# A layer's forward and backward pass on one core: the last stores on SyncE's queue, and the sines of the transform constants ahead of the exponential of dt

## The chip, the cores and the metric

The kernel runs on one core of a Trainium2 chip. The core has five engines, each with its own list of instructions that it works through in order: PE (TensorE, matmuls into PSUM), DVE (VectorE), ACT (ScalarE, with tables of functions that an instruction of its own loads), POOL (GpSimd) and SP (SyncE, which here only issues DMAs). Engines wait for each other through semaphores. DMAs are issued by SP, by ACT and by POOL; the profile counts what SP and ACT issue under the hardware queues and what POOL issues under the software queue.

The metric is the device time of one execution in microseconds, as the median of several runs. A trace of one profiled execution tells what each engine did; its span runs from the first to the last instruction.

## The reference

`A_u` is x, 2048 rows of 512 in bf16. It is normalised, run through a state space layer (a long convolution, computed by Fourier transforms) and gated by a feed-forward block; the kernel returns the output and the gradients of it towards eleven inputs.

```python
def _A_ref(u, A_re, A_im, B_re, B_im, C_re, C_im, log_dt, Dskip):
    dt = jnp.exp(log_dt)[:, None]
    A, Bc, Cc = A_re + 1j * A_im, B_re + 1j * B_im, C_re + 1j * C_im
    P = jnp.exp((dt * A)[:, :, None] * l[None, None, :])
    K = jnp.einsum("dn,dnl,dn->dl", Cc, P, dt * Bc).real
    # y = causal convolution of u with K along the rows, by rfft and irfft over 2L
    return y + u * Dskip[None, None, :]

def _B_ref(x, w1, w2):
    return silu(x @ w1) @ w2

xn = _layernorm(A_u)
out = A_u + _A_ref(xn, ...) * silu(_B_ref(xn, w1, w2))
# returned: out, and by jax.vjp with grad_out the gradients of
# A_u, A_re, A_im, B_re, B_im, C_re, C_im, log_dt, Dskip, w1, w2
```

## The kernel before

The function `body` (line 1488) writes the whole program down once in a plain order, through a recorder; nothing is issued yet. A plan then cuts it into 3232 steps (a step is one instruction, or a few matmuls of one group) and puts them into the sequence that is packed in the string `ORDER` (line 185): `solve` (line 421) unpacks it, `emit` (line 119) issues the steps in that sequence, and `tie` holds each engine to it. A number of `ORDER` also says whether a copy out of PSUM, or a row of the normalisation, runs on ACT or on DVE (the steps made with `any_copy` and `any_affine`). The order on each engine and each DMA queue is therefore written out by hand, step by step, and the line that issues nearly everything is one: line 171 of `emit`. That is why almost every row of the profile says L171. Line 1684 opens and closes the program; its rows are drains and semaphores.

**The start.** SP loads x (four pieces `x_sb` of 512 KB, `load_x`), the weights `W1` and `W2` (1792 KB each) and six parameters (`par_Ar`, `par_Ai`, `par_Br`, `par_Bi`, `par_Cr`, `par_Ci`, 128 KB each, by transposing DMA). ACT issues the loads of log_dt (`ldt`) and of Dskip (`Dbc`). Three chains begin there and share DVE:

- `make_consts` (line 546) makes the constants of the transform. `twiddles` multiplies two integer ramps into `prod` on DVE (a multiply and an addition, for each half) and ACT takes the sine into `TF`. PE transposes `TF` into `pt_t`, eight blocks at a time, and a copy brings each eight to `TI`; there are four such groups.
- `ssm_magnitudes` (line 801) takes dt = exp(ldt) on ACT, multiplies it with `par_Ar` on DVE (`lam` and the four parts of `lamr`), and takes 30 exponentials of `lam` and `lamr` on ACT into `mag_all`. SP stores that as eight blocks `Md` and later loads it back, block by block, as `mag`, where `gen_tables` needs it.
- `layer_norm` (line 656) takes the statistics of x on DVE (`st`, `mv`, `ve`), a power on POOL (`rstd`) and scales the rows (`xn`). Two rows at a time are transposed on PE and copied to `XT` on DVE, and with `XT` the feed-forward block begins: matmuls with `W1` into `ps_h`, copied out to `hT` by ACT or DVE, `aT` = silu on ACT, matmuls with `W2` into `ps_o`.

**The end.** The last stretch weaves three things: the gradients of `W2` and `W1` (`gen_dw2`, `gen_dw1`: matmuls into `ps_w`, copies to `o`, stores), the state space parameters' gradients of the last block, and the backward pass of the normalisation.

- `gen_ssm_grads` (line 1219) runs once for each of four blocks of 128 channels, in the order `k.back = 3, 0, 1, 2`, so block 2 is last. It computes six gradients into `gout` on DVE, transposes them on PE (`pt_g`), copies them back on ACT, and stores them in six pieces of 32 KB (line 1268). Then it stores the gradient of log_dt (`ddt`).
- `gen_ln_bwd` (line 1437) goes through the rows in eight pairs of 128, in the order `first` = 5, 6, 7, 0, 1, 2, 3, 4. For each it loads the incoming gradient `Gt` on SP, multiplies and adds on DVE, and stores `Gt`, 256 KB, at line 1475. Four buffers hold `Gt`.
- `gen_dw1` ends with four parts of the last piece of `W1`'s gradient, each of which is copied by ACT and stored on SP (`out_dram<-o`, 64 KB).

All other stores go through `k.st`, which is POOL's queue (line 1522): in the end six stores of `gout`, `ddt`, the last pieces of `o` and the `Gt`.

Of the kernel before, what the change touches and what calls it, by code (L numbers as in the profile page):

```python
# [180 lines left out]
class Plan:  # L181
# [1 line left out]

    ROOM, BOUND = 212832, 450.0
    ORDER = (
        "c-l>v4`|eBddHvVo!RL)J3BW!H#;}X&P}skI-8rF=5jWd%Vx7#n+s{0rfHg{Y3ijCLJ*NOwN`>i5D^<h775!RvMeIout?a7UAD4_h!v3_vWNt+RwOKTS"
# [3 lines left out]
        "x>*zQuyS2c$Ds)38bVgfPy-(kg>qxgo>z7vT(>K}g8f^_Zi|~9!?m)wGTek9EmN)1x`O{}|Rleg|Vc$0SxvZn#EUSMd=j0Eeg!}+o=IDD$vwIc`p2QQ5"  # L190
        "@s#0P9_xR>3TL>lqU}%Q8`>)C|Fe87|B9}2jK76U_vHxOe=bwHAwR;_XW_8`kLxn0O;AdH%&Z$SgPu$qJvy&;A4d}-I;#&Qtykds0lIu3c}9IJS$r-B4"
        "_VowTePhAWe@GK1bPedy>#jKGOe5Ss%+O9nz#TJeASC`Qy%MMe?HIrUAjxVbSG_xHo@H!#^;gnO=K(~Q4{wfZB;HySubncC0k+40sUI9=zTo^CGq_=9e"
        "}Sd;6AH+;nMW?Df?u&C*-0g#6~6L0RC0<w>BBooGu~dlD0B8!5V8ikEa~g<Gdy0YUtHtdIBGsm7Q{yzM1eQcA6#*TUp_BI85I+I;K_mTbYo-kYMg+yuL"
        "|Vh>|(2@U&U%YWH|VCv_V7(D^os%MxDo{A-yu4hIKyS#RrU=u4hIz&EdJXZTi2$bJQ>6Tx^qq7sh4MILX>Gxx`|gnX!<>OOi`(1%6lnQ%%^@x9?o30c%"
        "dRzDfCvJf(k2KJ?&ozLq%Jrbt04=m{So<8TQ1MlsI-X+#%bRjH+E*S_NvOS!4Y)BzT3h!Fib<KrbSl6!56|&(1D}SOR09X?INTQc3ZpD9-Q&I`1u;nRv"
        "s2_7pghHs(BYbU83I6XwD_V9fp2SXNz89UEXeHi`Vr@eKyY9zIXPvwK^u$G6yLa?u{9!{k7%4IxjMEgrnGA9Hn7-}o^-P~>a7nM|2vHjY4Nbo(zV)+8h"
        "h#&QXN%at&H_gPFQ|oDc&Z<%@s(rtvX(;+-(Q1@AW|NG*)E5WA`=X$Ucw^_VmdcYPho?T!Dc?j|10vRXuFS{he4{Gm|d5#Q&vvHWfwTI6@LB^ttWZwkW"
        "Q}c+yht@mq~Eyu<iln5_s#1F6fl(Ag(^rZE!FRHqYq}?uIi*`8ElegkzBDX@n+dG$#k~w?VW~05Sd(%_U_=*h5ssv3~&$s_>OV60_qfZ8$6tLxZ6|Y$I"
        "OI%D<z%G{_X#s|7OTOn?Xp`6sehvl&5_@bM+^%<SAIjbDLW(XgdOuEoBfmja%7N;B}B;z{Jb?nWzd_Y>nLj-GDwzMZdzEeW|nv)=@ooF-P1zKhBF-#X("
        "qPB`}^c>4g$P3VOCq>VX7Myhz89AK3iNZ(Eld{6d4bu2o=*AhB^o&B0Ua>n4RA|r5^1-JhKZz-bbKFIh>ql+G>UwXAy4@p0ntB0}OuJcazZO4k8P!l$`"  # L200
        "43{L^b!t0W*-oC^&R&!BZI_DTr&`iB>}jYmPL50?<CxO~JN;H((n;2RRevpi4ets0J!GoE-3IqtXf!1+d;ZI?=Z0hHE$00fJS6eB0oU(Uve71=8FMZE{"
        "6#zlq<u}Qk*0!2$1997e@@XhvEFs)`DnAuDYwvJS)?tn%K{jYL^BoWGLp`aCwI!6>}J&8v;OO}A$Iu@e5F}^KpW_D8_u_~!xFqMK!>23>+2WtHas36pK"
        "QTGTfpx))@_I0VucJ<PTcTV|4x3wdT+QlcIi7hftIUS^(C@*Qh(+cW7Nv?A7~0|JfXV!-myD@cDA}ljX(p$sKw$i^^4Ube?oi0w_jnCoAM=@`8WPuXyz"
        "f;U5{N(Z)4LgVq=h+=pEilAm1|H&<V2TxSIDjNzM`3Y7T2weY}B&%;TFFXMUE6@T~}MS^VpkBYVzqybP_;QfSir`kD;kql1omle8x6@HfoKz;DLu#zr3"
        "M^{aVIipVITS&LPR`X1)g;qGnMWd$ui&sM?pW4bH5Ph`QFA&;K|Ynd%=g%SBnua5c|(c`vBfQ=nom9PKN@D-><e#&zlzi7uR+QC<=wf4}ea24R^DD*xw"
        "h2Kmg%_aKA$m!=<>(@xN-=!I5&ImqSqVln<KZuPQUVE1BXCSMiK88LeBCT#-gpN92f%^D;>gZ$mnjyu4BgY~uuX<bMInFwVS*7Y8Xy|5|n5SNw=e|Uxy"
        "$gG#>7T_<H+=6!G4xG<Ux6=im$UBp*ubY9R7s}YK$X-lJM{urix!KNomQDi#<}h!XYO|Wn$~iz^Emxxjg&`XTFlz5_*tvR$tw4hXO?!~)BM1=tNF+jBe"
        "sDy2au?l{hR5@!_yGjn}gpX>)*$^1-K}|Wr0{sxFkt-!w<p93FeRcm=gWxeAO(xr(EAD`o_5y-M`X&zt8Fx4aW@w;mh!^H_C5GU$+iA<ULQexMZ7ou11"
        "t{Y)HFi;<PUOv6p)pkIf^i$(ZL1P^9noxehVA1-XjM75V}gQSc}!`8qpkR_P8>mAAS@CZHNS4tpg(%J;xqKQ=gm#>;Tr#g4X*tuhap3?1-qK5ckk^ZeT"
        "C=v!yCX1uEAvekTtl4Da}gd~q?C6}ipmcb37=iEkH;M7hk1?CN6sX=_*IIx<e$)nw>jTS>y*R7q7`nayjtHiCHk51BCmk$40bp7Rdw>o>#@q0pt`BHXW"  # L210
        "8<IT~tFoGy{W9z3oLjT)7`|M_ud9wZX_vg>r^6OT=g~;svFLTjytLOQt?nUPJdf5~s}t~L)pOb{VqSa4@wEbf=Bq`Y-M~u2vku2KleE>JvVKyUbZmLe`"
        "LOyR9U;zh>M<<!jBNI`N}|olxUT!md;X=$2*dm=TC?i5<kSpR82yCNBOtHUi{_z+u+l;7GUqtG3o7{OGf!UnA!O(~jhs`ilbY+!qUa~AbH;J9H{!@*Cx"
        "<55Bjnvgf2Yed=IiA>!Z%~>J~+v+cF|9LHiq*J^FZ5>W2chm0@LmQGt8H)8hEaUE<D|QeVVV0`Z42k^B!9#L1fFN?eJ0ub!yD~f$R6E=eaYC9D=5yIa)"
# [1475 lines left out]
```

## Time and profile before

| | us |
|---|---|
| median of 3 runs | 556.71 (556.11 to 558.98) |
| the profiled execution, its own time | 558.34 |
| the profiled execution, its span | 556.3 |
| PE busy, of the span | 514.4 |
| DVE busy | 514.9 |
| ACT busy | 432.8 |
| POOL busy | 69.8 |

The granted TensorE clock is 0.989 over the span. Busy time of PE is modelled from the starts of pipelined matmuls, so a busy PE isn't one at its peak. Register, branch, semaphore, drain and DMA-issuing instructions of the queues count as idle. A row of the timeline gives start, duration, engine, line, operation and what it writes and reads; "SPq" and "ACTq" are the issues of those engines' queues. In brackets stands how long the engine had been idle and what ended the wait.

### The profile page before, as it was taken

What the parts mean: (1) busy time and instruction counts of PE and PEld (TensorE: products, weight loads), DVE (VectorE), ACT (ScalarE), POOL (GpSimd) and SP (SyncE); (2) the same over time, 40 slices, a digit from 0 to 9 for tenths busy, and PEclk for the clock granted to TensorE, in tenths of its full rate; (3) what the DMA queues carried; (4) which work ended last, traced back from release to release, by engine and by line L of the source; (5) the groups of instructions that cost most, each with busy time, mean ns of one, the idle gap of its engine ahead of it and who ended that gap; (6) DMA issues with size and microseconds to landing.
All of it is one profiled execution on the core that took longest, in us unless ns stands there. A gap on an engine that the chain in (4) does not pass through costs nothing.

```text
span 556.3 us, 18980 instructions
## 1 busy us (share of the span) xinstructions
PE 514.4 (92%) x8173; PEld 368.1 (66%) x8173; DVE 514.9 (93%) x930; ACT 432.8 (78%) x707; POOL 69.8 (13%) x133
## 2 busy tenths in 40 slices
PE   0799989999979889879999999999999999999995
PEld 0566556767647657567686777777665667667774
DVE  8899998999989999999999999868999898899994
ACT  6999897999888869999999998564556656676533
POOL 3241210110000100000000000000000120403333
PEclk9999998999979999999999999999999999999999
DMA  8687775889897999967679977999999999999993
GB/s 269 222 334 194 264 281 182 257 292 230 206 290 237 229 351 338 192 187 134 209 248 227 333 236 265 230 256 238 270 228 235 237 241 225 234 219 235 246 222 138
DMA packets 169140, 134.41 MB, mean 242 GB/s; under 512 B 115552, under 2 KB 149088, under 8 KB 166496
## 3 DMA queue, kind: packets, MB, share of 16 engines
q1 hardware_dynamic: 162704, 115.36, 81.0%
q0 software_dynamic: 6064, 17.57, 8.8%
q8 instruction: 64, 1.05, 0.7%
q10 hardware_dynamic: 288, 0.26, 0.2%
q14 instruction: 20, 0.16, 0.1%
HBM read 49.28 MB, written 56.10 MB: 189 GB/s over the span
## 4 chain that ended last, share of the span: by engine, by line
PE 69%; DVE 14%; ACT 10%; issue 3%; DMA 3%; POOL 0%; ACTq 0%; DVEq 0%; POOLq 0%
PE ps_w L171 15%; PE ps_da L171 9%; PE ps_dx L171 9%; PE ps_i L171 8%; PE ps_h L171 6%; PE ps_s L171 5%; PE ps_o L171 5%; ACT dA L171 3%; PE ps_k L171 3%; PE psS L171 3%; PE pt_t L171 3%; DVE AR L171 2%; DVE YD L171 2%; DMA h_in<-Hd 2%; PE ps_v L171 2%
## 5 line engine op out<-in xcount | busy, mean ns | idle before, releaser
L171 PEld LDWEIGHTS <-W 128*128 128x128 bf16 x1008 | 92.2, 99 | 27.2 <-issue 4.4
L171 ACT CAST dA<-ps_s 128x512 bf16<-128x512 f32 x151 | 83.0, 627 | 9.0 <-PE ps_s L171 6.7
L171 ACT CAST Vb<-ps_v 128x320 bf16<-128x320 f32 x113 | 40.7, 441 | 34.4 <-PE ps_v L171 24.6
L171 PE MATMUL ps_h<-XT,W 128*128 128x256 bf16 x448 | 61.8, 284 | 0.9 <-DVE XT L171 0.7
L171 PE MATMUL ps_o<-W,aT 128*128 128x512 bf16 x224 | 60.3, 386 | 0.9 <-ACT aT L171 0.7
L171 PE MATMUL ps_da<-doT,W 128*128 128x256 bf16 x448 | 58.2, 273 | 0.0
L171 PE MATMUL ps_dx<-W,dhT 128*128 128x512 bf16 x224 | 58.1, 379 | 0.0
L171 PE MATMUL ps_w<-YD,a_tok 128*128 128x512 bf16 x224 | 56.6, 379 | 0.7 <-ACT o L171 0.7
L171 PEld LDWEIGHTS <-xn 128*128 128x128 bf16 x512 | 46.7, 98 | 14.5 <-DVE xn L171 4.5
L171 PE MATMUL ps_w<-dh_tok,xn 128*128 128x256 bf16 x448 | 56.0, 273 | 0.0
L171 DVE TENSOR_TENSOR Tp<-Vb,Eb 128x1280 bf16<-128x1280 bf16 x64 | 51.3, 818 | 2.5 <-ACT Vb L171 1.6
L171 ACT CAST dB<-ps_i 128x512 bf16<-128x512 f32 x82 | 44.1, 621 | 5.7 <-PE ps_i L171 5.7
L171 PEld LDWEIGHTS <-TF 128*128 128x128 bf16 x416 | 28.1, 99 | 19.9 <-ACT TF L171 11.4
L171 DVE TENSOR_TENSOR dhT<-ps_da,dhT 128x512 bf16<-128x512 f32 x56 | 37.2, 685 | 4.2 <-PE ps_da L171 2.0
L171 PEld LDWEIGHTS <-YD 128*32 128x32 bf16 (+1 forms) x2112 | 25.0, 103 | 16.5 <-issue 14.5
L171 ACT CAST o<-ps_w 128x512 bf16<-128x512 f32 (+1 forms) x30 | 16.4, 559 | 23.6 <-PE ps_w L171 11.8
L171 ACT CAST hT<-ps_h 128x512 bf16<-128x512 f32 x49 | 28.5, 622 | 5.5 <-PE ps_h L171 5.3
L171 PE MATMUL ps_s<-dB,F 128*64 128x512 bf16 x192 | 29.7, 396 | 2.6 <-DVE dA L171 1.3
L171 PE MATMUL ps_k<-W,YD 128*32 128x20 bf16 x2048 | 26.2, 204 | 5.7 <-issue 5.3
L171 PEld LDWEIGHTS <-aT 128*128 128x128 bf16 x224 | 19.3, 98 | 17.6 <-issue 4.1
L171 PEld LDWEIGHTS <-a_tok 128*128 128x128 bf16 x224 | 20.1, 98 | 16.3 <-issue 0.6
L171 POOL DMA_DIRECT2D Hd<-hT x16 | 14.1, 884 | 130.5 <-ACT hT L171 126.1
(234 smaller groups left out, 1162.8 us busy)
## 6 DMA issues: line engine op xcount, KB each, us to landing
Yd<-YD SPq DMA_DIRECT2D x8, 1024.0 KB
Ed<-E SPq DMA_DIRECT2D x8, 640.0 KB
Eb<-Ed SPq DMA_DIRECT2D x8, 640.0 KB
h_in<-Hd SPq DMA_DIRECT2D x10, 512.0 KB
Hd<-hT POOLq DMA_DIRECT2D x8, 512.0 KB, 6.7
dhT<-Hd SPq DMA_DIRECT2D x8, 512.0 KB
DHd<-dhT SPq DMA_DIRECT2D x8, 512.0 KB
Md<-mag_all SPq DMA_DIRECT2D x8, 480.0 KB
```

The lines of the kernel that those rows point to most:

```text
L171: getattr(getattr(nc, engine), op)(*[on(a) for a in args], **{w: on(a) for w, a in kw.items()})
```

## The change

Two stores get another queue, and the sequence is another one in two places. The packed string is new as a whole; its lines can't be read, so only its first and last are shown, and what is in it follows as lists.

```diff
     ORDER = (
-        "c-l>v4`|eBddHvVo!RL)J3BW!H#;}X&P}skI-8rF=5jWd%Vx7#n+s{0rfHg{Y3ijCLJ*NOwN`>i5D^<h775!RvMeIout?a7UAD4_h!v3_vWNt+RwOKTS"
...
-        "L!sUZu>@FY}hjEXWp!1wViMhuIGeTq#4(5{6*exitg#?%$1CA$i^fiUPb;FsX9pN"
+        "c-l>v4`|eBddHvVo!Pl@c6N4lc6M%<olfVxbS^hL&F0cHm(AsJHkYQkG-thBnx<YVX$TS|4c1CnB!~nFR*ofz?1?NA77-Co?6N0|h*%L3k!7(W)-EDew"
...
+        "EP96f%jRowH?|9<$PDR8-arNNIE*_Bc#cCMiF=YCjGSAyur)3j>Y}-#SLk5bnvyB77@2Y^Y_01-%Pj"
     )
@@ gen_ssm_grads
     for i in range(6):
-        k.st(k.outs[2 + i][bs, :], outb[:, i])
+        (nc.sync.dma_start if b == k.back[-1] else k.st)(k.outs[2 + i][bs, :], outb[:, i])
@@ gen_ln_bwd, rows
-        k.st(k.o1_v[:, 2 * c:2 * c + 2, :], Gt[:])
+        (nc.sync.dma_start if c in first[-2:] else k.st)(k.o1_v[:, 2 * c:2 * c + 2, :], Gt[:])
```

**The first 331 steps** are the same set in another order; the start of each engine's list:

```
ACT before: ldt, Dbc | dt=exp | TF=sin | TF=sin | 25 x mag_all=exp | hT | 5 more mag_all ...
ACT after:  ldt, Dbc | TF=sin | TF=sin | dt=exp | TI<-pt_t | 25 x mag_all=exp | hT | 5 more mag_all ...

DVE before: p_h p_t p_t pj | prod kk prod | sh kq kq | prod prod | pj st | lamr sh lam kq mv lamr st lamr mv lamr
            | st p_e st mv sp_dBr mv | TI<-pt_t | st st mv mv ve ...
DVE after:  prod prod prod | p_t p_h | prod | p_e p_t | st kk mv sh st kq pj mv sh kq pj st kq st kf mv mv
            | lam st lamr lamr lamr lamr ecst mv st maskf ve | mv sp_dBr st ...

SP before:  x_sb Ar x_sb Br Ci x_sb Bi W1 Cr x_sb W2 Ai | 8 x Md, then mag
SP after:   x_sb x_sb Ar x_sb Br x_sb W1 Bi Ai Cr Ci W2 | 8 x Md, then mag

PE before:  TF group | xn group | TF group | 12 steps of ps_h | xn group | TF group ... | TF group
PE after:   TF group | TF group | TF group | xn group | 10 steps of ps_h | xn group | a step of ps_h | TF group ...
```

The new sequence puts five steps on the other engine of the two: a copy of `TI` (DVE to ACT), a row of `xn` (ACT to DVE), and three copies of `hT` (two ACT to DVE, one DVE to ACT; one of the two that come to DVE stands behind the row `AR<-ph,ecst`). PSUM buffers are handed out by the sequence, so many tiles get another number of the same eight.

**The end.** Behind step 331 the sequence is the same but for the six stores of `gout` of the last block, which now stand directly behind ACT's copy of `gout`. With the new queues, the lists end so:

```
SP before:   ... dh_tok | Gt load (c=3) | Gt load (c=4) | o | o | o | o
SP after:    ... dh_tok | 6 x gout | Gt load (c=3) | Gt load (c=4) | Gt store (c=3) | o | o | o | o | Gt store (c=4)
POOL before: ... gout o o gout o gout Gt Gt ddt o gout Gt gout Gt gout
POOL after:  ... o o o Gt Gt ddt o
```

More of the change, by code (lines that the diff above doesn't have):

```diff
@@ L190 @@
[L190 to L213, printed above, removed]
@@ new lines @@
+        "=SFT3R<IUxTft=cW$QX4HYN7>7&|0zRo`T;T;4alE6<#bq{OI53Sh<;n;OPQs14z2ab9W6>ha+0T1<*1hBp8Q7Vbx?l5_?^gJktJ=BC$g7WF4K2HbMk$"
+        "7zlkO$bV85lCfTLCGzopl+;NTTq-5nTnwdb4IcY<#y!<hoe#x^>Tl5kCIe80>T&LGPbY7OCwrhiNC0f?yqCAu@c&kVTT^6N7y0Bw`dESPz4C4#*ZAF8x"
+        "(ktr{T;rL6vWz-_XPlBxC<o-9(bzHUe1`RJW98q<A+5k!oYmjNzAb3%807&nPU{0{hm*Ygn|v3aD8kP*iZE+l2DPL&<WuA}UUuo4?9{Aof!64iN25j7$"
+        "YZHTl2uXTDk~k@p=EtY|A$Bxs4d7>(xYF=v~JX^vQ6vqIo^3e3bf^r{idwzy1$=i{0`lrJvvL-u2rn`l>T|-{GO!Y>;yGw)=eYpWhv`rHE+wItvvF4p;"
@@ new lines @@
+        "z>w?uC+YcTI=j>l0mo>)mjfrr&8bt>w_iMNNqHO5jWTu!nuM%c$mb1qoNQjj;*lxTXtu;eLIeuY_C;{rVnWkkC2&>MV6L;d}VaG<I)ehLd4Gb-&j!t;y"
+        "fw5yK(D*o}Bk75l|y9$QrTvZwvWBRYmHruC@vZ4{RkozWMqWy&}l?9;<~M^8eZ@_tB<>kaJ=kF<pBSCBdpjK>2i;Q(CZWdX~U<qtf<kLqcCm)hg#qr%E"
+        "(!m6%n-u)>{`?4-G`>~Lf#gJiavt^K#&+9!s5T<kh?;Z4-0q3gA@t{|JEI*PNT?~t%M}|U|YzyaU>murtl(TY6Z)q;%!Y%CyJs}$|F!KrB5`^|TrB$xD"
+        "6@QC&R>CT_T$LyKA<sl8ga$Q2Ym-Xw|2cG=*flL4!%k(|i%wPdV3C7ZJCEPla}QQJ>)h?3CNARIy{j+d5BK%H8fH!h<1_{6Btu+2q;4B)J=f<NT+%DLg"
@@ new lines @@
+        "?Nq;*{0tVZG+6xCD~BpJ%Qf@Ru(u4ctJhX!!!LrjjtS|4{JH}(f$Thlpn&AVeAr8WP-)`OL$~KOy|bwDmFM4Y~(urUy+}o?EzNa4D#m0?0OhGW#uGX_J"
+        "FaQ;O8IFy5U<FsMrI7bP;#mtUO7??$=$i3m#|D+@em&cH-&--3kZOpy#|A*4IFTgS1UTCgB)ldfGw}$Ebby+c4TF$hYNR(Ogothh0Qf9QzmGpr(d>FFE"
+        "#~qHGR}#L#dU3|onpv+^%!FU<}VSgRGPK?x8cA^)U@!6f^w;NvUup4+)S+RX~=7EN1P<XY?tdNDLy)eJnRcoTW3JJCwq{lvJ5qo+H3Z==<)B_W?t>^Ff"
+        "Xr-_xMuVS+Pht9Z-6V81J-VR|o!}@sC=RMg>#1x<*X0ctbll|`}@-EcCqBFFX(D|FJ*W!^g245A~qK3||veOOHYhDK+<1dXa`k+DS*M40BXZfOUuj{;<"
@@ new lines @@
+        "bvv<QH&n&Od!QuyXt#Evm2EOb>B3G){ws=~g3|5S(@<la{V0u$V@?yS^gr?v`;*9P`YZWscu&Z;kf{!L_xZn#MpN=KmMh_ZJzkfiHZA`S4@o?3$n|@b9"
+        "chD)jJXzn@J&1hq<uqbk*0!2$1C(Qe@;<0Fy9U6MQ^jrs#|EkEK?R)Wf6=>qL~VG8A)g43f?-;ejJy7VE#8LBdqdm_)0VTkT%ih4xDddg%x;RgqEPX>+"
+        "4VD9eCW!e$s)3I>7HZ*6oDeVup<Tns4w}|BhYn75R>PV~_qwC(v>YtG*;{?C)<o#u&Bn{zsa^8c)egzH;nNpq)+bQCpxPV$@=Bv;36$e)$W^Q`&xtO>V"
+        "M>ej@+v?LsjRx#4>3ae4=v_7EGx@|Pg#JD!Cd#v8gpwj59M{%Vx9<lxkbWij7DL+0^S`k9|)B77^tTNeMi?Z}>U94|wbccjpy`So=f!AFN3^(HA*?C>{"
@@ new lines @@
+        "^RS6?PnJGc!Y~+O$Z#t(kiHoQABDQs^>cFhBK3Efxf#P{E$i8k!N(WED7cl=>vqc%?G{TRp$UE6Bh2>8PFW5cJYG_czaz4yDZdr1`PujZy|#zZaNqA0b"
+        "ACT&`CXcMK?l4s$@=XP<<R50z9C=BbILQB3QeCiosWmF{r<sDrFJ&?zMpg(@<<y|meLXZ*W9<-<fhjBuJud(Oq>38Q?JTneatE7)98k1-0z6S?ab*Mg6"
+        "7DdXBQuZyUn(5>JhyNak|qBJcl?Dr}UiO@O!r$XcJVJ?UwdChUPtg?3M*An9x1?F4T%A$2DLNQgnS^?PlXSGOlR$o7~^zOcMFyx>5GfV<&Shkqvf}-#w"
+        "JIh!Re1e!F5G^M#XTz(w@g$qFrzWO@E;o^xE{6xF<?&Z^~WmnrjV-%mX^%8*U<Ax$p`Qq-d6y)H-O4#D3Ou@dl<qi*k8_`+>Q-jmNjl{K=?IByAkOzr="
```

36 lines of the change are left out of this document (20 added, 16 removed).

## The prediction

> **What bounds the kernel now.** I read the page first, for the engines' shares.
>
> ```profile
> span 556.3 us, 18980 instructions
> ...
> PE 514.4 (92%) x8173; PEld 368.1 (66%) x8173; DVE 514.9 (93%) x930; ACT 432.8 (78%) x707; POOL 69.8 (13%) x133
> ```
>
> PE and DVE are both nearly full over the whole span, so a gain has to come from a place where something stands still. The change touches two such places, the first 50 us and the last 20. For the first I read a window:
>
> ```profile
> 12.00:20.00 8.00, 2.97 (x24) 2.35 (x23) 7.53 (x24) 7.99 (x16) 1.89 (x6) 1.00 1.06 395
> ```
>
> The columns are the stretch, its length, then busy time of PE, PEld, DVE, ACT and POOL, the clock, the DMA share and GB/s. PE waits while DVE and ACT are full and the DMA engines are busy throughout. The chain of waits says what opens the kernel:
>
> ```profile
> 0.80 4.83 DMA ldt<-in_A_log_dt_dram
> ...
> 19.31 7.32 PE ps_h L171 x40
> ```
>
> It begins with the load of log_dt, and the first real matmuls run at 19.31. Between them stands ACT, whose timeline I read next:
>
> ```profile
> 1.71 1.28 ACT L171 ACT_TABLE_LOAD   x1 [1.71 <-PEq L1673]
> 5.65 0.63 ACT L171 ACTIVATE dt<-ldt 128x512 bf16<-128x512 bf16 x1 [2.66 <-DMA ldt<-in_A_log_dt_dram]
> 6.30 1.28 ACT L171 ACT_TABLE_LOAD   x1
> 7.59 3.71 ACT L171 ACTIVATE TF<-prod 128x2048 bf16<-128x2048 int16 x2
> 11.32 1.28 ACT L171 ACT_TABLE_LOAD   x1
> 12.62 0.63 ACT L171 ACTIVATE mag_all<-lam 128x512 bf16<-128x512 f32 x1
> ...
> 27.08 0.58 ACT L171 CAST hT<-ps_h 128x512 bf16<-128x512 f32 x1 [1.37 <-PE ps_h L171]
> ```
>
> ACT loads a table, stands 2.66 us for log_dt, takes one exponential, loads the sine's table, makes both halves of TF, and loads the exponential's table again for the 30 exponentials of mag_all: three loads in 12.6 us, one of them only because the first exponential stands ahead of the sines. Yet ACT isn't the engine that decides here, for DVE is as full. All that DVE waits for up to 44.3 us, by the waits view:
>
> ```profile
> DVE hT L171 <- PE ps_h L171: 1.7, 3, 0.7
> DVE p_h L171 <- POOL ip L171: 1.2, 1, 1.2
> DVE TI L171 <- PE pt_t L171: 0.5, 1, 0.5
> DVE lamr L171 <- DMA par_Ar<-in_A_A_re_dram: 0.5, 1, 0.5
> DVE dA L171 <- PE ps_s L171: 0.2, 1, 0.2
> ```
>
> That is 4.1 us in 44.3, and no reordering can give DVE more than that without taking work from it.
>
> For the end I read the rows of line 1684, the program's closing (its drains and semaphores; start of the first and last in us, durations in ns):
>
> ```profile
> L1684 POOLq EVENT_SEMAPHORE  x4: 17/17/17, 555.5 to 556.2; - x4
> L1684 POOLq DRAIN  x3: 40/102/6354, 549.1 to 556.0; - x3
> L1684 SPq DRAIN  x3: 7/7/13, 552.1 to 555.7; - x3
> ```
>
> POOL's first drain takes 6.354 us, 549.1 to 555.5. SP has seen every store land and drains at 552.1, then stands 3.4 us. So **what ends last is POOL's drain**, not the last matmul and not the last store. What it has to close over:
>
> ```profile
> 544.61 0.79 POOL L171 DMA_DIRECT2D out_dram<-o  x1
> ...
> 549.15 0.54 POOL L171 DMA_DIRECT2D out_dram<-gout  x1 [0.21 <-issue]
> ```
>
> The last POOL store is issued until 549.69, 5.8 us before the drain ends.
>
> **The head, part by part.** On ACT the sines come first, then dt, then the exponentials. The multiplies that feed the sines now open DVE's list:
>
> ```profile
> 1.56 1.22 DVE L171 TENSOR_TENSOR prod<-il,jf 128x1024 int32<-128x1024 int32 x1
> ...
> 2.94 0.79 DVE L171 TENSOR_SCALAR prod<-prod 128x1024 int32<-128x1024 int32 x1
> ...
> 6.11 0.68 DVE L171 BATCH_NORM_STATS2 st<-x_sb 128x6 f32<-128x512 bf16 x1
> ...
> 7.51 1.01 DVE L171 TENSOR_TENSOR lam<-dt,par_Ar 128x512 f32<-128x512 bf16 x1
> ...
> 12.43 0.69 DVE L171 COPY TI<-pt_t 128x1024 bf16<-128x1024 bf16 x1 [0.47 <-PE pt_t L171]
> ...
> 16.96 0.37 DVE L171 TENSOR_SCALAR xn<-x_sb,rstd,nb 128x512 bf16<-128x512 bf16 x1
> ...
> 44.22 0.81 DVE L171 TENSOR_TENSOR AR<-ph,ecst 128x640 int32<-128x640 f32 x1
> ```
>
> They start some 0.3 earlier, so the first half of prod is there at about 1.25 + 1.22 + 0.79 = 3.3 us and the second 2.0 to 2.2 later, at 5.5. ACT: first sine 3.3 to 5.2 (3.71 / 2 each), second 5.5 to 7.4, one table load to 8.7, dt to 9.3. dt is thus 3.0 us later than before (6.28). On DVE the multiply lam, which needs dt and began at 7.51, now stands behind three more bn_stats of 0.68, at about 9.5: the later dt is hidden by work that had to be done anyhow. lam takes 1.0, and mag_all starts near 10.4 instead of 12.62: ACT is **2.2 us ahead**. A second step of ACT, the copy of TI, moves over from DVE and fits in the 1.1 us between dt and lam. The wait of 1.37 at 27.08 can go too, since the copy of hT that waited is DVE's now and another one stands later: ACT's lead is then 2.2 + 1.4 = 3.6.
>
> PE: its first transposes of TF come sooner, into its idle time, and cost nothing there. POOL's fills are permuted in time in which it waits. PSUM buffers get other numbers, in the same sequence of use behind step 330. SP: its 12 loads are permuted. par_Ar stands behind one more x_sb (512 KB, 1.3 us at the 395 GB/s above) and lands near 8.5, ahead of the 9.5 at which it is wanted. If that cover went, each us would push lam, and with it DVE, by as much.
>
> DVE decides. It loses the waits on pt_t, par_Ar and ps_s, 0.5 + 0.5 + 0.2 = 1.2; it gets one of about 0.3, at its first bn_stats: it is there near 5.65, two small steps behind the second prod, and the rows of x_sb were there at 6.11, so 0.5 at most. Work: without the copy of TI, 0.69, with a row of xn that was ACT's, 0.37: 0.3 less. Two copies of hT change places between ACT and DVE and cancel. At the row of 44.22 that makes 1.2 - 0.3 + 0.3 = **1.2 us ahead**. Behind it DVE gets one more copy of hT that was ACT's; nearest row the copy of 0.69. That bounds the lead at 0.5 from below if nothing hides it. From above: all waits but the first 1.2 gone, 2.9 + 0.3 = 3.2. I take 1.2, DVE's own lead at the last common point; behind step 330 every engine's list is as before, so a lead that all engines have is kept to the end.
>
> **The tail, part by part.** Eight stores move from POOL to SP: six of gout (the last block, b = 2) and the Gt of c = 3 and 4. The six stand on SP directly behind the last transposing load, ahead of the last two loads of Gt.
>
> ```profile
> 535.68 1.01 SPq L171 DMA_DIRECT2D Gt<-in_grad_out_dram  x2
> 545.13 5.53 SPq L171 DMA_DIRECT2D out_dram<-o  x4
> ```
>
> ```profile
> 58.86 0.34 SPq L171 DMA_DIRECT2D Yd<-YD  x1
> ```
>
> ```profile
> 537.28 0.79 ACT L171 COPY gout<-pt_g 128x768 bf16<-128x768 bf16 x1
> ...
> 549.92 0.37 ACT L171 CAST o<-ps_w 128x256 bf16<-128x256 f32 x1 [0.94 <-PE ps_w L171]
> ```
>
> ```profile
> 543.80 1.40 DVE L171 SCALAR_TENSOR_TENSOR Gt<-xn,m,Gt 128x512 bf16<-128x512 bf16 x2
> ...
> 547.42 0.69 DVE L171 TENSOR_TENSOR Gt<-Gt,AR 128x1024 bf16<-128x1024 bf16 x1
> ```
>
> ```profile
> out_dram<-Gt POOLq DMA_DIRECT2D x4, 256.0 KB, 3.1
> ...
> out_dram<-gout POOLq DMA_DIRECT2D x6, 32.0 KB, 2.1
> ```
>
> The added wait: SP stands for gout until 538.07, and the two Gt loads wait behind it. An issue took SP 0.34 us for a store (Yd) and 0.5 for a load of Gt; at 0.4 with the gap behind it the six are out at 540.5 and the loads at 541.5, against 536.7 before. DVE wants the first at 543.80, the second two us later; 3.1 us after issue they land at 543.6 and 544.6. So this is just hidden, and if it is late by half a microsecond only the Gt branch moves, whose last step ended at 548.11, 2.5 us ahead of SP's last o store. The end is still PE, ACT until 550.29, and SP's last o store, issued until 550.66, as before. Behind it SP now issues the last Gt store, until 551.05. Before, SP was done 1.45 us after its last issue; a store of 256 KB takes 3.1 - 2.1 = 1.0 longer than a small one (POOL's own rows). So SP is done at 551.05 + 1.45 + 1.0 = 553.5. POOL's last store is now the o of 544.61, issued until 545.40; its drain, at 5.8 behind the last issue, ends at 551.2, and if it runs from the landing instead (551.25 to 555.5, 4.25) at 544.61 + 3.1 + 4.25 = 552.0. Either way **SP is what is late next**. From 555.5 to the end the closing took 0.8: 553.5 + 0.8 = 554.3, **2.0 us less**. Bounds: without the extra 1.0, 3.0; with a drain that doesn't move at all, 0.
>
> A rule of the Trainium skill speaks against this part. "DMA: Bandwidth & Descriptors", section "Issuing engines are not separate DMA queues", says that DMAs from any engine run on the same 16 DMA engines and that spreading them over issuers saves only the issue time. The row of POOL's drain says that here POOL's closing comes 3.4 us behind SP's. By the rule alone the tail would give nothing, and the sum would be the head's 1.2.
>
> **Sum.** 1.2 + 2.0 = 3.2. The profiled execution took 558.34 with a span of 556.27, so 2.07 lie around it: 553.1 and 555.1. The median of the runs shown is 556.71, 1.6 below that execution, and I forecast against it: 556.7 - 3.2 = **553.5**, own range 552.0 to 555.0.
>
> **The rivals.** *DVE eats the lead.* DVE waits 0.6 more at each of two first evictions, or for lam; the head gives 0. For it: DVE waits for only 4.1 us of its first 44.3, and it gets a copy more. Against: 1.2 us of its waits have no cause any more. Time 556.7 - 2.0 = 554.7.
>
> *PE wakes sooner.* The first matmuls run at half pace, whatever the clock column says:
>
> ```profile
> 19.30:25.10 5.80, 5.79 (x28) 1.00 0.63 174
> 25.10:27.30 2.20, 2.20 (x22) 1.00 0.00 0
> ```
>
> 28 in 5.80 us, 207 ns each, then 22 at 100. The slow stretch costs 28 x 107 ns = 3.0 us, and the 1.7 us that DVE waits for ps_h come from it. If it is shorter after the earlier start, those 1.7 go: head 2.9, time 551.8. Against: nothing in the trace says what ends the stretch. "TensorE: Matmul & The Clock Gate", "Part 1: The HAM clock gate", of the Trainium skill gives about 3.4 us of sustained work before full rate, in free-running windows; the row shows 5.8. By that figure the stretch would be 2.4 shorter and the sum, as an estimate, 1.2 larger, 552.3.
>
> *The drain follows the last landing of any queue* and ends on the other side. Place: POOL's drain. Price: the Gt store on SP lands about 553.2, the drain ends 4.25 later at 557.45, the end is 558.25, 2.0 later, less the head's 1.2: 557.5. It decides from a last landing later than 551.25 + 1.2 = 552.45. Against it: SP's queue and POOL's are separate, and a drain that closes POOL's descriptors has no reason to wait for SP's. For it: the trace has only one such drain.
>
> *The head doesn't do what it says*: W1 stands behind 256 KB more (one x_sb more, two parameters fewer), 0.65 us; it was there by 19.31 at the latest, so by 20.0 at the latest, wanted near 18. Two us late, head -0.8, 555.5.
>
> **How the numbers follow.** About half a per cent, 2.8 us, is what a measurement of this kernel can tell from no change; the border is 553.9. Forecast 0.55, most of it (0.38) under the border; DVE eats the lead 0.18; PE wakes sooner 0.13; the drain follows any landing 0.08; W1 late 0.06. Faster 0.38 + 0.13 + 0.01 = 0.52, slower by over 0.5% 0.02, the same 0.46. The range takes in the forecast, PE's early wake and the tail alone: 551.2 to 556.2.
>
> **What would show it.** ACT: two table loads ahead of the first mag_all, which starts near 10.4. The first ps_h near 18. The row AR<-ph,ecst near 43. SP: six gout stores from 538 on, the last Gt store last. POOL's long drain shorter or, if not, starting some 4 us sooner, and over before SP's. Wrong would be: a long drain that still ends last; a DVE wait over 0.5 us at lam or at the last two Gt; AR<-ph,ecst no earlier than 44.

## The result, and the profile after

The changed kernel takes **553.75 us**, the kernel before, measured in the same series, 559.14 (medians of 20 runs each); the ratio is 0.9918, with a 95% interval of 0.989 to 0.9946. It counts only the executions within 1.5% of each kernel's fastest, so it isn't the quotient of the two medians. The changed kernel is faster by 0.82%, or 4.6 us (3.0 to 6.2). A second series on another occasion gave 0.9877 (0.9819 to 0.9934). The forecast was 553.5 us and 3.2 us less than before. Both are near what came out, but the kernel before was also 2.4 us slower over 20 runs than over the three on which the forecast stood, and the gain came out 1.4 us larger: that 553.5 lies so close to 553.75 is luck, and the gain is the number to compare.

What follows is the profile of a second execution of the changed kernel (a2 below), with a span of 548.4 us; the first one is "after" in the table below, with a span of 557.6. The end first, by the rows of the closing, the timeline of the queues, and the timeline of ACT:

```profile
L1684 POOLq DRAIN  x3: 40/93/6712, 539.0 to 548.1; - x3
L1684 SPq DRAIN  x3: 7/7/13, 547.6 to 547.9; - x3
```

```profile
532.53 2.72 SPq L171 DMA_DIRECT2D out_dram<-gout  x6
535.35 0.87 SPq L171 DMA_DIRECT2D Gt<-in_grad_out_dram  x2
541.47 0.34 SPq L171 DMA_DIRECT2D out_dram<-Gt  x1
541.91 3.18 SPq L171 DMA_DIRECT2D out_dram<-o  x4
545.18 0.38 SPq L171 DMA_DIRECT2D out_dram<-Gt  x1
...
539.04 0.79 POOL L171 DMA_DIRECT2D out_dram<-o  x1
...
544.36 0.37 ACT L171 CAST o<-ps_w 128x256 bf16<-128x256 f32 x1 [0.94 <-PE ps_w L171]
```

POOL's long drain still takes 6.7 us, but it starts at 539.0 and is over at 545.7. SP closes later, at 547.6, 2.0 us behind its last Gt store (issued until 545.56), and 0.8 later the span ends. The last copy of `o` on ACT ends at 544.73 and the span 3.65 behind it; in the profile of before these were 550.29 and 556.27, so 5.98. **From the last result on ACT to the end the change saves 2.3 us** in this execution. In the first profile it doesn't; the section on SP's order at the end shows why.

The head, by the timelines of ACT and DVE:

```profile
1.73 1.28 ACT L171 ACT_TABLE_LOAD   x1 [1.73 <-PEq L1673]
3.26 3.77 ACT L171 ACTIVATE TF<-prod 128x2048 bf16<-128x2048 int16 x2 [0.25 <-DVE prod L171]
7.05 1.28 ACT L171 ACT_TABLE_LOAD   x1
8.34 0.63 ACT L171 ACTIVATE dt<-ldt 128x512 bf16<-128x512 bf16 x1
8.88 0.99 ACT L171 COPY TI<-pt_t 128x1024 bf16<-128x1024 bf16 x1
11.55 2.71 ACT L171 ACTIVATE mag_all<-lam 128x512 bf16<-128x512 f32 x5 [1.68 <-DVE lam L171]
```

```profile
7.04 0.69 DVE L171 BATCH_NORM_STATS2 st<-x_sb 128x6 f32<-128x512 bf16 x1 [1.83 <-DMA x_sb<-in_A_u_dram]
...
10.53 0.99 DVE L171 TENSOR_TENSOR lam<-dt,par_Ar 128x512 f32<-128x512 bf16 x1
...
43.65 0.81 DVE L171 TENSOR_TENSOR AR<-ph,ecst 128x640 int32<-128x640 f32 x1
```

Two table loads stand ahead of the first `mag_all`, not three, and it starts 1.07 us sooner (12.62 before). DVE reaches `AR<-ph,ecst` at 43.65 instead of 44.22. All that DVE waited for up to there, and its busy time up to that row, before and after (windows from 0 to the row; columns: length, then busy time and count of PE, PEld, DVE, ACT, POOL, then clock, DMA share, GB/s):

```profile
DVE st L171 <- DMA x_sb<-in_A_u_dram: 1.8, 1, 1.8
DVE nb L171 <- POOL rstd L171: 1.3, 3, 0.7
DVE prod L171 <- POOL jf L171: 1.3, 1, 1.3
DVE hT L171 <- PE ps_h L171: 0.8, 1, 0.8
```

```profile
0.00:44.22 44.22, 27.67 (x225) 20.66 (x226) 39.91 (x121) 38.35 (x60) 15.63 (x41) 1.00 0.82 276
```

```profile
0.00:43.65 43.65, 28.26 (x226) 21.12 (x228) 38.39 (x119) 37.88 (x57) 16.72 (x42) 1.00 0.87 288
```

Not what the forecast summed. DVE stands *longer* than before (43.65 - 38.39 = 5.3 us against 44.22 - 39.91 = 4.3), and works 1.5 us less.

### The profile page after: what moved, and what is told of

Its sections match the earlier page's. It is cut to its first block, busy times and chain, and to the rows that moved or that the text cites. A ratio compares the mean times of both kernels' runs of the same rounds, so it can differ in the third digit from the quotient of the medians.

```text
span 557.6 us, 18927 instructions
## 1 busy us (share of the span) xinstructions
PE 509.4 (91%) x8121; PEld 368.1 (66%) x8173; DVE 514.2 (92%) x931; ACT 431.2 (77%) x705; POOL 66.5 (12%) x125
## 4 chain that ended last, share of the span: by engine, by line
PE 35%; DMA 10%; issue 7%; DVE 5%; ACT 5%; POOL 1%; SPq 0%; DVEq 0%; ACTq 0%; POOLq 0%
PE ps_da L171 9%; PE ps_dx L171 8%; PE ps_w L171 5%; PE ps_i L171 5%; DMA out_dram<-gout 3%; DMA Gt<-in_grad_out_dram 3%; PE ps_s L171 2%; PE psS L171 2%; ACT dA L171 2%; DMA h_in<-Hd 2%; PE pt_t L171 1%; DMA Pd<-pd_s 1%; PE ps_v L171 1%; DVE dA L171 1%; POOL out_dram L171 1%
## 5 line engine op out<-in xcount | busy, mean ns | idle before, releaser
L171 PE MATMUL ps_o<-W,aT 128*128 128x512 bf16 x194 | 53.9, 380 | 1.9 <-issue 1.0
L171 PE MATMUL ps_w<-YD,a_tok 128*128 128x512 bf16 x202 | 53.1, 379 | 2.1 <-ACT o L171 0.8
L171 PEld LDWEIGHTS <-ident 128*128 128x128 bf16 x404 | 25.8, 98 | 6.8 <-DVE Tp L171 2.7
L171 PEld LDWEIGHTS <-dhT 128*128 128x128 bf16 x224 | 19.9, 98 | 14.6 <-issue 1.1
```

What stands on the lines that cost most here:

```text
L171: getattr(getattr(nc, engine), op)(*[on(a) for a in args], **{w: on(a) for w, a in kw.items()})
```

## The experiments

Twelve more runs were made, in three series: nine other kernels, and three repeats for a second profile (a2, b2, the second of before, and e1b). In each, "of before" is the ratio to the kernel before of the same series, with its 95% interval; 0.5% is 2.8 us. Since the sequence is a packed string, the edits are shown as the lists that changed.

Two quantities are read off a single profile: the row `AR<-ph,ecst` (the head), and the stretch from the start of SP's last `o` store to the span's end (the tail). The second is short and repeats well. The first scatters by 1.3 us between profiles of one head, mostly with "PE slow": how long the first matmuls into `ps_h` start 213 ns apart, before they start 109 ns apart. All fourteen profiles, with the granted clock between 82 and 88 us and the first row of `YD<-sy,mag` behind 90 us, of which more below:

| profile | head | tail | of before | PE slow | AR row | clock 82–88 | YD row | last o to end |
|---|---|---|---|---|---|---|---|---|
| before, first | old | old | 1 | 5.7 | 44.22 | 0.72 | 96.38 | 5.95 |
| before, second | old | old | 1 | 3.6 | 43.51 | 1.00 | 94.22 | 5.95 |
| e2 tail only | old | new | 0.9964 (0.9927–1.0) | 4.2 | 43.88 | 0.50 | 97.46 | 3.65 |
| e1 head only | new | old | 0.9957 (0.9926–0.9989) | 2.9 | 42.73 | 1.00 | 93.22 | 5.72 |
| e1b, the same | new | old | – | 5.7 | 44.04 | 0.72 | 95.69 | 5.73 |
| after | new | new | 0.9918 (0.989–0.9946) | 3.8 | 43.14 | 1.00 | 93.35 | 3.78 |
| a2, the same | new | new | 0.9877 (0.9819–0.9934) | 5.1 | 43.65 | 1.00 | 94.45 | 3.63 |
| e4 loads first | new | SP reordered | 0.9907 (0.9869–0.9945) | 5.1 | 43.48 | 1.00 | 93.75 | 2.65 |
| e7 one on POOL | new | one Gt on POOL | 0.9952 (0.9914–0.999) | 5.5 | 43.90 | 0.72 | 95.45 | 5.71 |
| e8 gout on POOL | new | six gout on POOL | 0.9908 (0.9872–0.9943) | 4.7 | 43.70 | 0.75 | 95.01 | 3.83 |
| e6 par_Ar second | loads exchanged | new | 0.989 (0.9843–0.9937) | 5.1 | 43.00 | 1.00 | 93.14 | 3.63 |
| e9 both | loads exchanged | SP reordered | 0.9898 (0.9857–0.994) | 5.7 | 43.22 | 0.72 | 95.16 | 2.66 |
| e5 swap only | old, tables swapped | old | 1.0017 (0.9974–1.006) | 4.6 | 46.00 | 0.72 | 97.93 | 5.92 |
| e3 dt first | new, tables not | new | 1.0001 (0.9955–1.0048) | 4.9 | 47.56 | 1.00 | 97.93 | 3.61 |

### The changed kernel again

> The changed kernel once more, for a profile of an ordinary execution beside the four kernels of the first series. If its end is as it was in the kernel with the exponential of dt first (same tail): POOL's drain ends 2.5 to 2.6 us behind the landing of POOL's last o store and about 2 us ahead of SP's; the span ends 3.6 us behind the start of SP's last o store, where the kernel before needed 5.9. Time against before: 0.992, as measured already.

Its profile is the one shown above: the drain 545.7 against SP's 547.6, the span's end 3.63 behind the start of SP's last `o` store. The tail is that of e3, as expected.

### The two halves apart

e1 is the kernel before with the first 331 steps in the new order, e2 the kernel before with the new queues and the new order at the end.

```diff
 e1:  first 331 steps
-  the order of before
+  the order of after
      the rest, queues of all stores: as before
 e2:  first 331 steps: as before
-  the rest, queues: as before
+  the rest, queues: as after
```

> The kernel before with the first 331 steps in the new order; the rest of the list and the queues of all stores as before. If the head's gain is a lead that every engine keeps (the forecast's reason, now put at 1.1 us, the shift of the row AR<-ph,ecst from 44.22 to 43.14): that row starts near 43.1, POOL's long drain still ends last, and everything at the end comes 1.1 us sooner, about 555.6 where the kernel before has 556.7. If DVE eats the lead (rival): AR<-ph,ecst near 43.1 all the same, but the tail where it was, within 0.4 of before. If the whole gain of the change (4.6 us of 559) comes from the head: about 552.

> The kernel before with the new tail alone: eight stores on SP's queue and the new order of the steps behind 525 us; the first 331 steps as before. If the drain of POOL was what ended last and SP's last store ends next (the forecast's reason): POOL's drain over 1 to 3 us ahead of SP's, 1.5 to 2.5 us less than before. If the six gout stores that stand ahead of the last two Gt loads on SP cost as much as the drain gave (DVE waits for these loads for 1 to 2 us each, and SP's last o stores stand behind a Gt store that waits): within 0.7 us of before. If the drain follows the last landing of any queue: slower than before by 1 us or more.

Measured: head alone 0.9957, 2.4 us less (0.6 to 4.1); tail alone 0.9964, 2.0 us less (0 to 4.1). The two add up to 0.79%, close to the 0.82% of the whole. The closing rows, of e1 and then of e2:

```profile
L1684 POOLq DRAIN  x3: 40/93/6444, 547.2 to 554.2; - x3
L1684 SPq DRAIN  x3: 7/7/13, 550.6 to 553.9; - x3
```

```profile
L1683 POOLq DRAIN  x3: 40/102/6694, 548.1 to 557.2; - x3
L1683 SPq DRAIN  x3: 7/7/13, 556.7 to 557.0; - x3
```

In e1 POOL's first drain ends at 547.2 + 6.4 = 553.7, 3.1 behind SP's: the old picture. In e2 it ends at 548.1 + 6.7 = 554.8, 1.9 ahead of SP's 556.7: the new one. In this profile the tail doesn't give back on SP what it saves; e2's time alone, whose interval reaches 1.0, wouldn't exclude it. The rival in which DVE eats the lead, with a time within 0.4 us of before, is out by e1's interval.

### One store back on POOL, and six

e7 puts the last of the eight stores back on POOL's queue, e8 the six of `gout`.

```diff
 e7, gen_ln_bwd:
-    (nc.sync.dma_start if c in first[-2:] else k.st)(...)
+    (nc.sync.dma_start if c == first[-2] else k.st)(...)
 e8, gen_ssm_grads:
-    (nc.sync.dma_start if b == k.back[-1] else k.st)(...)
+    k.st(...)
```

> The changed kernel with one of the eight stores back on POOL's queue: the last Gt store, 256 KB, the other seven stay on SP. If POOL's drain runs some fixed time behind POOL's last store (2.6 us behind its landing or 5.8 behind its issue, by the runs so far): the store is issued near 549, lands near 551.5, the drain ends near 554.5 and is last again, the time 1.0 to 2.0 us above the changed kernel. If the number of POOL's stores or their kind sets the drain, one store among eight costs little: within 0.4 of the changed kernel, or less than it, since SP then ends with an o store.

> The changed kernel with the six gout stores back on POOL's queue, in the new order of the list, so that they stand early on POOL (from 537 on); the two last Gt stores stay on SP. If only a late last store on POOL costs, and not how many stores POOL has: POOL's last store is still the o near 544 to 546, its drain over before SP's, the span's end 3.6 us behind the start of SP's last o store; the Gt loads, no longer behind gout on SP, are issued near 537 and DVE doesn't wait for them. Time within 0.5 of the changed kernel. If the six on SP were worth something by themselves: 1 us or more above the changed kernel.

```profile
L1683 POOLq DRAIN  x3: 40/102/5795, 551.9 to 558.2; - x3
L1683 SPq DRAIN  x3: 7/7/13, 554.8 to 558.0; - x3
```

```profile
551.95 0.54 POOL L171 DMA_DIRECT2D out_dram<-Gt  x1 [4.08 <-DVE Gt L171]
...
552.79 0.33 SPq L171 DMA_DIRECT2D out_dram<-o  x1
```

These are e7's rows. One store issued on POOL at 551.95 brings the whole old end back: POOL's drain is last again, 551.9 + 5.8 = 557.7, and the span ends 5.71 behind the start of SP's last store. In the time that is 0.9952 against 0.9877 of the changed kernel in the same series, and above its 0.9918 in the first; the intervals overlap a little, so it is the rows that carry this. e8, with six stores more on POOL but all of them early (536.54 to 539.75), is as good as the changed kernel, 0.9908, and its drain is over at 549.8, 1.3 ahead of SP's. So **it is one late store on POOL that costs, not how many POOL issues**; in the new order the last Gt store alone decides. (That store moved by itself in the old order, where `gout` is late on POOL too, wasn't tried.)

### SP's order at the end

```diff
 e4, SP's list:
-  dh_tok | 6 x gout | Gt load | Gt load | Gt store | o | o | o | o | Gt store
+  dh_tok | Gt load | Gt load | 6 x gout | o | Gt store | o | Gt store | o | o
```

> The changed kernel with the order of SP's queue alone changed: the last two Gt loads ahead of the six gout stores, and the last o stores in the order in which their copies come, between and behind the last two Gt stores. If SP's head of line is a cost of the changed kernel (in its profile DVE waits 1.99 and 0.31 us for these loads, and o stores copied from 546.4 on are issued from 552.3): no DVE wait over 0.3 us for Gt, SP's last store about 2 us sooner, 1 to 2 us less than the changed kernel. If the loads were just hidden, as the forecast had it, and SP's last store is set by PE and ACT: within 0.4 of the changed kernel.

The forecast held the two Gt loads for "just hidden". In the changed kernel they aren't (DVE's row of a2), in e4 DVE doesn't wait; the second fence is the end of SP's list in e4:

```profile
539.24 1.41 DVE L171 SCALAR_TENSOR_TENSOR Gt<-xn,m,Gt 128x512 bf16<-128x512 bf16 x2 [0.94 <-DMA Gt<-in_grad_out_dram]
```

```profile
547.75 0.38 SPq L171 DMA_DIRECT2D out_dram<-Gt  x1
548.22 1.62 SPq L171 DMA_DIRECT2D out_dram<-o  x2
```

DVE loses 0.94 us, in e4 nothing. In a2 that wait isn't on the path: both kernels end behind ACT's last copy. In the first profile of the changed kernel ("after") it is. DVE waits 1.99 and 0.31 us for the two loads there, and this is SP's list behind them:

```profile
551.90 0.34 SPq L171 DMA_DIRECT2D out_dram<-Gt  x1
552.34 1.85 SPq L171 DMA_DIRECT2D out_dram<-o  x4
554.42 0.33 SPq L171 DMA_DIRECT2D out_dram<-Gt  x1
```

ACT's last copy of `o` ends at 551.50, but the four `o` stores stand behind a Gt store that SP can't issue before 551.90, and the last Gt store waits for DVE until 554.42. From ACT's last copy to the end of the span it takes 6.1 us, as long as in the kernel before: in that execution the tail's saving was gone, though POOL's drain was over before SP's. SP came free of the last transposing load (`dh_tok`) only at 541.72 there, 2.4 us behind ACT's copy of `gout`; in a2 it was free 2.4 us ahead of that copy. How often this happens the runs don't tell; of the five profiles with this order on SP it is one.

What e4 gains is that an `o` store of 64 KB is last on SP, not a Gt store: SP closes 1.5 us behind its last issue instead of 2.0, and no store stands behind the last `o`, 2.65 from its start to the end instead of 3.63. In the time this 1.0 doesn't show, nor what it would save in executions like the one above: 0.9907 against 0.9918, within both intervals.

### The two sines and the exponential

e5 makes the swap alone in the kernel before; e3 undoes it alone in the changed one.

```diff
 e5, ACT's list (all else as before):
-  ldt Dbc | dt=exp | TF=sin | TF=sin | mag_all ...
+  ldt Dbc | TF=sin | TF=sin | dt=exp | mag_all ...
 e3, ACT's list (all else as after):
-  ldt Dbc | TF=sin | TF=sin | dt=exp | TI | mag_all ...
+  ldt Dbc | dt=exp | TF=sin | TF=sin | TI | mag_all ...
```

> The kernel before with one step moved on ACT: the exponential of dt behind the two sines; every other engine's list as before, the loads too. If the order of the tables by itself gives the head's gain: mag_all starts near 10.5 instead of 12.6 and the time falls by 1 to 2 us. If DVE decides (the forecast's reason): DVE stands for dt at lamr and lam from 7.2 on until about 10, some 2.5 us, so AR<-ph,ecst comes 1 to 2.5 us later than 44.2 and the time is the same or up to 2.5 us more, because the new order of DVE, which fills that wait with statistics, is missing.

> The changed kernel with one step moved back: on ACT the exponential of dt again ahead of the two sines, so that ACT loads a table three times ahead of mag_all. If the order of the tables is what gives the head's gain: mag_all starts near 12.6, AR<-ph,ecst back near 44.2, 1.1 us above the changed kernel. If DVE's own list decides and ACT only has to be not too late (the forecast took the gain from DVE's lost waits for pt_t, par_Ar and ps_s): AR<-ph,ecst stays near 43.1 to 43.4 and the time within 0.4 of the changed kernel, because DVE's waits for ACT stay small with mag_all 2 us later.

DVE in e5, then ACT in e3:

```profile
10.05 0.29 DVE L171 TENSOR_TENSOR lamr<-dt,par_Ar 128x128 f32<-128x128 bf16 x1 [3.26 <-ACT dt L171]
```

```profile
7.25 0.63 ACT L171 ACTIVATE dt<-ldt 128x512 bf16<-128x512 bf16 x1 [4.24 <-DMA ldt<-in_A_log_dt_dram]
7.90 1.28 ACT L171 ACT_TABLE_LOAD   x1
9.19 3.71 ACT L171 ACTIVATE TF<-prod 128x2048 bf16<-128x2048 int16 x2
14.03 1.01 ACT L171 COPY TI<-pt_t 128x1024 bf16<-128x1024 bf16 x1 [1.13 <-PE pt_t L171]
15.06 1.28 ACT L171 ACT_TABLE_LOAD   x1
16.35 2.71 ACT L171 ACTIVATE mag_all<-lam 128x512 bf16<-128x512 f32 x5
```

e5 saves a table load and starts `mag_all` at 11.37, yet DVE stands 3.26 us for dt, and everything behind is late: AR at 46.00. The time is 1.0017, no gain. The swap is worth nothing by itself, in the old order of the other engines. e3 says the converse, and more than was expected: with dt first, the changed kernel comes to AR at 47.56, 3.9 us behind a2, and its time is 1.0001, the whole gain gone: 0.83% above the changed kernel's 0.9918, 4.6 us. My expectation that ACT "only has to be not too late" was wrong, because I had overlooked that log_dt itself is later in the new order: it landed at 5.65 before and lands at 7.25 here. In the changed kernel nobody sees that, since the sines fill the time; with dt first all of ACT waits for it. Then the copy of `TI`, now ACT's, waits for sines that are late, and `mag_all` behind it starts at 16.35. **The parts of the head hold each other up; neither order of the tables is good in the other's list.**

### Which load stands second

Why is log_dt later, and why does DVE wait 1.83 us for its first piece of x, where the forecast gave 0.3?

```diff
 e6, SP's list:
-  x_sb | x_sb | par_Ar | x_sb ...
+  x_sb | par_Ar | x_sb | x_sb ...
 e9:  this and the edit of e4
```

> The changed kernel with two loads exchanged on SP: par_Ar again second and the second x_sb third, as the kernel before had them. The changed kernel's first x_sb lands at 6.8 and log_dt at 7.0, where they landed at 5.9 and 5.6 before, and DVE waits 1.6 for the first x_sb. If the second x_sb delays the first by sharing the DMA engines: first x_sb near 5.9, DVE's wait 0.7 to 0.9, lam and mag_all 0.5 to 0.9 sooner than the changed kernel's 10.3 and 11.3, AR<-ph,ecst about 0.5 sooner; in the time 0.5 to 0.9 less than the changed kernel, or nothing if DVE waits for the second x_sb instead. If the wait has another cause (the first multiplies' place on DVE): the wait stays at 1.6.

> The changed kernel with both repairs that the runs so far suggest: SP's last two Gt loads ahead of the six gout stores and the o stores in the order of their copies, and par_Ar ahead of the second x_sb. From the rows: 1.0 us at the end (SP's last o store to the span's end 2.6 instead of 3.6), 0.5 to 0.7 in the head. If both are kept to the end: 1.5 us less than the changed kernel, about 0.985 to 0.988 of the kernel before. If the head's part is taken back by a later wait: 1.0 less. If the span's end hangs on something else: within 0.4 of the changed kernel.

```profile
6.22 0.69 DVE L171 BATCH_NORM_STATS2 st<-x_sb 128x6 f32<-128x512 bf16 x1 [1.02 <-DMA x_sb<-in_A_u_dram]
...
9.86 0.99 DVE L171 TENSOR_TENSOR lam<-dt,par_Ar 128x512 f32<-128x512 bf16 x1
```

With `par_Ar` second again, the first piece is there at 6.2 instead of 7.0, DVE's wait is 1.02 instead of 1.83, lam 0.67 sooner, AR at 43.00. This repeats: the first piece of x lands at 5.8 to 6.4 in the six profiles with `par_Ar` second, and at 6.8 to 7.1 in the eight with another `x_sb` second. So a load of 512 KB that is issued 0.45 us *behind* another one makes the first land 0.8 later: the queue doesn't finish the one before it begins the next. In the time the 0.65 isn't seen: 0.989 against 0.9877 in the same series. e9, with both repairs, gives 0.9898: by its rows 1.0 less at the end and 0.4 in the head than a2, by its time the same. **None of the variants beats the changed kernel by more than the measurement resolves.**

### The dip at 82 us

The first profiles suggested that the new head did one thing more: with the old head the granted clock fell between 82 and 88 us, DVE then waited 1.4 to 3.4 us for ACT's `sy` near 96, and with the new head it mostly didn't.

> The kernel before once more, for a second profile. In the first, as in the two others that have the old head and in one of the new, the granted clock falls to 0.5 to 0.9 between 82 and 88 us, and DVE then waits 1.4 to 3.4 us for ACT's sy near 96. If the dip belongs to the old head: a dip and a wait of 1.5 us or more here too. If it comes and goes from one execution to the next: either may be seen, and the 2 us that a profile with it loses at 96 are no part of what the new head gives.

> The new head with the old tail once more, for a second profile. AR<-ph,ecst between 42.7 and 43.7, as in the four profiles of the new head so far. If the new head keeps the clock from falling at 82 to 88 us: 1.00 throughout and a DVE wait under 0.7 us for sy. If the dip comes and goes: it may be seen here, with a wait of 1.4 us or more.

The windows from 82 to 88 of the two profiles of before, and then of e1 and e1b, which are one kernel (the clock is the third from the end):

```profile
82.00:88.00 6.00, 5.14 (x118) 3.46 (x119) 6.00 (x6) 2.76 (x5) 0.42 (x1) 0.72 0.31 126
```

```profile
82.00:88.00 6.00, 5.95 (x132) 4.13 (x133) 6.00 (x7) 4.19 (x8) 0.83 (x1) 1.00 0.39 148
```

```profile
82.00:88.00 6.00, 6.00 (x100) 4.29 (x86) 6.00 (x7) 4.45 (x7) 0.83 (x1) 1.00 0.33 114
```

```profile
82.00:88.00 6.00, 5.67 (x122) 3.88 (x124) 6.00 (x6) 2.40 (x6) 0.83 (x1) 0.72 0.29 116
```

The idea falls: the dip comes and goes with both heads, in seven of the fourteen profiles. What stays is the comparison of like with like, with one profile of the old head on each side, so it is a hint. Without the dip the row YD stands at 94.22 with the old head and at 93.22 to 94.45 (mean 93.7) with the new one, 0.5 sooner. With a dip to 0.72 or 0.75 it stands at 96.38 and 95.01 to 95.69 (mean 95.4), 1.0 sooner: then DVE waits for ACT, 2.0 us before and 1.2 to 1.5 with the new head. In pairs that also have about the same PE slow stretch it is 0.7 sooner (before, first, and e1b) and 0.9 (before, second, and after).

## Why the forecast came out, point by point

**What bounds the kernel: right.** POOL's drain ended last; e2 and e7 show it from both sides, taken away and put back.

**The tail: right in its mechanism and within 0.3 in its size, but not in every execution.** Forecast 2.0, by the rows of a2 and e2 2.3, by e2's time 2.0 (0 to 4.1). There SP is what is late next, and the end is still ACT's last copy and SP's stores behind it. Two terms were off. The Gt store at the end costs 0.5 more than an `o` store (2.0 behind its issue against 1.5), not 1.0. And the two Gt loads aren't just hidden: DVE waits 0.94 us for them, more than the 0.5 that the forecast named as its sign of error. In a2 that moves only the Gt branch, as the forecast also said, for that branch had 2.5 us to spare; in "after", with 1.99 and 0.31, the branch used them up and decided the end. That SP's `o` stores stand behind a Gt store, and so behind DVE, was not in the forecast's path. The forecast left open whether the drain runs from the last issue or the last landing, and both of its numbers were good enough, since either was ahead of SP.

**The rule of the Trainium skill** in "DMA: Bandwidth & Descriptors", "Issuing engines are not separate DMA queues", by which the tail would give nothing, doesn't hold for the end of this program: the tail is worth about 2 us, and one store decides it. The rule is about transfers, and nothing is transferred while POOL's drain runs on; in the kernel before, from 552.0 on, the DMA share and the GB/s (the last two columns) are zero:

```profile
552.00:555.40 3.40, 0.00 (x0) 0.00 (x0) 0.00 (x0) 0.00 (x0) 0.00 (x0) 0.81 0.00 0
```

**The head: right in direction, wrong in its sum.** The forecast was 1.2 us at `AR<-ph,ecst`, reckoned as 1.2 of DVE's waits lost, 0.3 of a new wait, 0.3 of work. At that row the seven profiles of the new head stand at 43.52 in the mean (42.73 to 44.04), the three of the old one at 43.87 (43.51 to 44.22): 0.35, below the lower bound of 0.5 and within the scatter. Pairs with about the same PE slow stretch give 0.2 (before, first, and e1b) and 0.4 (before, second, and after). The step that failed is the new wait at the first `bn_stats`: 1.8 instead of 0.3. I took the landing of x from the old list, 5.9, though another 512 KB now stands right behind it, and DVE is there at 5.2 and not at 5.65. `lam` then begins at 10.53 instead of 9.5 with dt ready at 8.97, so ACT's lead at `mag_all` is 1.1 and not 2.2; and ACT's wait for `ps_h`, which the forecast let go, is still there in a2 (1.31 against 1.37). A second wait was not in the sum at all, `nb` for POOL's `rstd`, 1.3. On the other side DVE waits 0.9 less for `ps_h`, which comes and goes with the PE slow stretch (0.8 in the second profile of before, 1.7 in the first), and its work up to that row took 1.5 us less, not 0.3. Only 0.6 of that is the copy of `TI`; the steps that both orders have took some 1.1 us less, so the bound that no order gives DVE more than its waits was too narrow. Why they are shorter stays open. The errors nearly cancel.

**"A lead that all engines have is kept to the end": neither shown nor refuted in its size.** e1's time says 2.4 us (0.6 to 4.1), the rows say 0.2 to 0.4 at 44 us and 0.5 to 1.0 at 95 us. These agree at the lower end of the interval only. ACT's lead at `mag_all` is 1.1, and where the clock dips DVE waits for ACT, so that part of it counts; where the rest of e1's gain arises, if it is there, stays open. Beyond 100 us single profiles can't tell, for two executions of one kernel drift apart by more than what is sought (below).

**The rivals.** *DVE eats the lead* (554.7): half true at the row AR, not in the time. *PE wakes sooner*: not because of the new head. The first `ps_h` start sooner (18.93 in a2, 19.31 before), but how long they run at half pace changes from one execution to the next. The matmuls into `ps_h` on PE, slow stretch and then fast, in the kernel before and in e1; and the slow stretch in e1b, the same kernel as e1 (the columns are PE busy and count, clock, DMA share, GB/s):

```profile
19.31:25.02 5.71, 5.71 (x27) 1.00 0.64 176
25.02:27.30 2.28, 2.28 (x22) 1.00 0.00 0
```

```profile
18.78:21.72 2.94, 2.94 (x15) 0.50 0.97 305
21.72:24.57 2.85, 2.85 (x27) 1.00 0.77 270
```

```profile
19.01:24.72 5.71, 5.71 (x27) 1.00 0.84 290
```

It lasts 2.9 to 5.7 us in the fourteen profiles, 4.5 in the mean with the old head and 4.7 with the new one, so it is no part of the gain; but a short one does bring `AR<-ph,ecst` forward, as the rival said (42.73 in e1, 44.04 in e1b). In e1 the clock column shows what the stretch is, a granted clock of 0.50; in the other profiles it reads 1.00 over the same half pace, so it can't be trusted there. "TensorE: Matmul & The Clock Gate" of the Trainium skill, "Part 1: The HAM clock gate", gives about 3.4 us for it; the rows show 2.9 to 5.7. *The drain follows the last landing of any queue*: no, in a2 POOL's drain is over at 545.7, while SP closes over its stores until 547.6. *W1 late*: no, `ps_h` starts sooner than before.

## What to carry to other kernels

The queue whose engine closes slowest should issue its last store early: look at the closing rows of every queue, not only at the last store, and move the one late store rather than all. Then look at what stands behind a moved store on its new queue: one that waits for its data holds up the stores behind it. When loads are put in another order, work out every landing anew, also those of loads that stand ahead of the one that moved. And a swap on one engine pays only if the engines that wait for it get an order to match: test the halves apart before crediting either.

## What the runs showed that I had not expected

**POOL's drain has two lengths.** In the five profiles in which POOL's last store is `gout` (32 KB), the first drain ends 5.79 us behind the end of that issue, each time to the hundredth, whatever the landing (4.1 to 4.2 behind it). In the eight in which it is `o` (256 KB), it ends 5.1 to 6.8 behind the issue, but 2.58 to 2.61 behind the landing in seven of them (2.8 in e8). In e7, with a Gt store last, it is 5.2 and 3.5, which fits neither. What sets the length stays open; that it follows POOL's own last store, and not SP's, is shown.

**A later load delays an earlier one on the same queue**, by 0.8 us for x (landed at 7.0 in a2, 6.2 in e6), and it delays log_dt, which another engine issues, by 0.7 (7.2 and 6.5).

**Executions of one kernel drift.** Matched row by row, the second profile of before is 4.5 us ahead of the first at 200 to 325 us and 1.3 at the end. PE's slow first stretch lasts from 2.9 to 5.7 us, half of the profiles have the clock dip at 82 us, and more dips follow, in a2 one at 236 us and in e1b one at 513. A difference of 1 us in the head can't be followed through one profile; it takes a short stretch in which both ends can be read, or many runs.
